# Transposing K on VectorE in place, in 32x32 blocks of element pairs, with block-diagonal queries and one score bank per pair

## Chip, cores and metric

The kernel runs on one core of a Trainium2 chip. The metric is the device time of one execution in microseconds, a median over several executions.

## The reference

Two layers share one K/V cache. Each is attention of one new token per batch row over 8192 cached keys, with a residual, then a silu feed-forward with a residual. A layer norm stands before each part.

```python
B, Sq, D = 8, 1, 512
Hq, Hkv, Sk, Dh = 32, 8, 8192, 128            # 4 query heads share a KV head
# all arrays bf16; F = 1792

q = (x @ wq) as heads
scores = einsum("bhqd,bhkd->bhqk", q, k) * (Dh ** -0.5)
o = einsum("bhqk,bhkd->bhqd", softmax(scores), v)
attention = o @ wo

x = x + attention(layernorm(x));  x = x + silu_ffn(layernorm(x))
x = x + attention(layernorm(x));  x = x + silu_ffn(layernorm(x))   # same K, V, weights
```

K and V of one batch row and KV head (a "pair") are 2 MB each. There are 64 pairs, each used in both layers, so 128 visits.

## The kernel before

The core does the batch rows in an interleaved order. K and V come in units of 512 KB (a quarter of a pair each) into an arena in on-chip memory, and a few units of each row are kept from the first layer for the second. Four "slots" make a pair, one per unit of K. Between the slots, the steps of a row's projection, feed-forward and next queries (a "middle") are slipped in, one step at a time. A helper records every read and write of a buffer and emits the waits.

```python
UNIT = 2048; NUNIT = 23; NKTR = 2; KEEP = 16
# ... cut ...
def k_src(b, g, q):
    return A_k_cache[b, g].rearrange("(p c) d -> p c d", p=128)[:, 16 * q:16 * q + 16, :]
def v_src(b, g, q):
    return A_v_cache[b, g].rearrange("(p c) d -> p c d", p=128)[:, 16 * q:16 * q + 16, :]
# ... cut ...
def layernorm():                                  # twice in each middle
    # ... bn_stats, bn_aggr on DVE, cut ...
    op(pool, lambda: pool.tensor_scalar(ve[0:B, :], mv[0:B, 1:2], LN_EPS, None, op0=ALU.add), ...)
    op(pool, lambda: pool.tensor_tensor(rstd[0:B, :], ve[0:B, :], mhalf[0:B, :], ALU.pow), ...)
# ... cut ...
def do_transposes(n, q):                          # a unit of K, as 1024 pairs of bf16
    # ... choice of the destination, kept unit or ring, cut ...
    src = unit(u).bitcast(FP32)
    for half in range(2):
        mm([lambda m=m: pe.transpose(TP[half][:, 128 * m:128 * m + 128],
                                     src[:, (4 * half + m) * 128:(4 * half + m + 1) * 128], ident[:, :])
            for m in range(4)], reads=[r_unit[u], res("ident")], writes=[r_TP[half]])
        if half == 0:
            op(dve, lambda: dve.tensor_copy(o, i), reads=[r_TP[half]], writes=[r_half, r_dst])
        else:
            op(act, lambda: act.copy(o, i), reads=[r_TP[half]], writes=[r_half, r_dst])
    free.append(u)

def do_scores(n, q):                              # 4 matmuls of 512 keys, 8 query columns
    # ... cut ...
    pe.matmul(SC[bk][32 * j:32 * j + 2 * REP, :], Q[:, b, g, e, :],
              kv[:, i * 512:(i + 1) * 512, e], start=(e == 0), stop=(e == 1))

def do_exp(n):
    # nb = -scale * max, on DVE, cut
    for t in range(2):                            # two score banks per pair
        op(act, lambda t=t, bk=bk: act.activation(P[:, t, :], SC[bk][:, :], ACT.Exp,
               bias=nb[:, :], scale=SM_SCALE, accum_out=ss[:, t:t + 1]), ...)

def do_pt(n):
    # 8 matmuls P x selection -> PTP; DVE copies PTP to PT; 2 f32 matmuls sum the sums; DVE: rz = 1 / sum
def do_pv(n, v):
    # 4 matmuls PT x V unit -> PV, accumulated over the four units
def do_norm():
    op(act, lambda: act.activation(E[:, :], PV[:, :], ACT.Copy, scale=rz[:, :]), ...)
def do_combine(n):
    # 4 f32 matmuls, 8 PE instructions: add the four partial outputs
    op(dve, lambda: dve.tensor_copy(attn[:, g * REP:(g + 1) * REP, b], MISC[:, 0:REP]), ...)

for slot in range(4 * NP + V_LAG + 1):            # program order of one slot
    # pump(): issue every load whose unit is free
    # scores of the slot before (plus max, exp at a pair's end), a middle step,
    # transposes of this slot, a middle step, P's transposition (slot 2), PV, norm, combine
```

## Time and profile before

| | before |
|---|---|
| median when the prediction was made (3 runs) | 1968.27 us |
| profiled span, mean granted TensorE clock | 1936.7 us, 0.904 |
| distance of the all-reduces in quiet pairs (the pair time) | 13.6 to 13.7 us |
| extra time of one middle | 26 us |
| bytes loaded | 481.9 MB |

The prediction below shows the lines that carry its argument. The groups of before's page give, after the bar, busy time and mean ns of one instruction, then the idle time before them and what ended most of it. The exp of 512 scores takes 682 ns, and the f32 combine is a group of 1024 PE instructions, eight per pair:

```profile
L643 ACT ACTIVATE P<-SC,nb 128x512 bf16<-128x512 f32 x256 | 173.5, 682 | 362.4 <-DVE junk L634 276.9
...
L693 PE MATMUL MISC<-selc,E 128*128 128x4 f32 x1024 | 138.6, 259 | 3.3 <-DVE hsT L512 2.5
```

The view of windows gives each engine's busy time in a stretch, then the granted TensorE clock, the DMA share and the rate. One quiet pair (one without a middle's steps and without kept units) of before has PE busy for 9.62 of 13.66 us, at the full clock:

```profile
1000.00:1013.66 13.66, 9.62 (x87) 5.97 (x86) 5.26 (x14) 4.27 (x9) 0.37 (x1) 1.00 0.94 351
```

### The profile page before, as it was taken

The numbers are of one execution on the slowest core, as the hardware profiler recorded it, in microseconds if no ns is written. First come the engines' busy times: TensorE is split into PE (matmuls) and PEld (weight loads), VectorE is DVE, ScalarE is ACT, GpSimd is POOL, SyncE is SP. The second block draws the span as 40 slices with busy tenths as digits, with TensorE's granted clock in tenths as the row PEclk, the third lists the DMA queues.
The fourth block names the chain that finished last, engine by engine and source line by source line (L and its number), as shares of the span: only waits on it lengthen the run. The fifth ranks groups of instructions, "written<-read, shape, count | busy, mean of one in ns | idle before, by whom it ended". The sixth has DMA issues, their size and how long they took to land. (4 is left out here: it accounts for less than half of the span.)

```text
span 1936.7 us, 30341 instructions
## 1 busy us (share of the span) xinstructions
PE 1373.5 (71%) x11410; PEld 822.5 (42%) x11410; DVE 701.5 (36%) x1789; ACT 542.7 (28%) x1150; POOL 64.9 (3%) x174
## 2 busy tenths in 40 slices
PE   3776787677767677766777767767676767767776
PEld 1444344444444344443444444444444444444443
DVE  3333333333333333333333323333333333333332
ACT  1332223322232223232233323332223322322331
POOL 0000000000000000000000000000000000000000
PEclk9998879988999888997899978899799988997997
DMA  9975697756977569765796658966598756855970
GB/s 380 374 268 167 214 352 258 235 163 218 383 251 235 179 234 371 235 220 180 261 390 220 214 162 313 339 224 205 167 337 326 241 164 209 301 176 185 361 277 1
DMA packets 135408, 483.84 MB, mean 250 GB/s; under 512 B 14417, under 2 KB 20321, under 8 KB 135009
## 3 DMA queue, kind: packets, MB, share of 16 engines
q1 hardware_dynamic: 135264, 481.89, 71.9%
q8 instruction: 94, 1.54, 0.3%
q14 instruction: 50, 0.40, 0.1%
HBM read 481.83 MB, written 0.01 MB: 249 GB/s over the span
## 5 line engine op out<-in xcount | busy, mean ns | idle before, releaser
L574 PE MATMUL TP<-ident,arena 128*128 128x128 f32 x3584 | 551.3, 303 | 0.0
L574 PEld LDWEIGHTS TP<-ident,arena 128*128 128x128 f32 x3584 | 436.2, 154 | 221.7 <-issue 221.7
L599 PE MATMUL SC<-ktring,Q 128*8 128x512 bf16 x1536 | 258.1, 418 | 328.2 <-ACT ktring L585 325.8
L585 ACT COPY ktring<-TP 128x512 int32<-128x512 int32 x384 | 224.4, 584 | 796.1 <-PE PV L677 368.7
L583 DVE COPY ktring<-TP 128x512 int32<-128x512 int32 x384 | 263.7, 687 | 345.2 <-PE TP L574 345.0
L612 DVE TENSOR_REDUCE m<-SC 128x1 f32<-128x512 f32 x256 | 176.8, 690 | 327.2 <-PE SC L599 327.1
L643 ACT ACTIVATE P<-SC,nb 128x512 bf16<-128x512 f32 x256 | 173.5, 682 | 362.4 <-DVE junk L634 276.9
L677 PE MATMUL PV<-arena,PT 128*16 128x512 bf16 x2048 | 231.1, 410 | 10.7 <-PE PV L677 0.3
L599 PEld LDWEIGHTS SC<-ktring,Q 128*8 128x8 bf16 x1536 | 37.4, 83 | 423.0 <-ACT ktring L585 418.4
L693 PEld LDWEIGHTS MISC<-selc,E 128*128 128x128 f32 x1024 | 127.5, 196 | 32.8 <-DVE rz L664 27.5
L693 PE MATMUL MISC<-selc,E 128*128 128x4 f32 x1024 | 138.6, 259 | 3.3 <-DVE hsT L512 2.5
L599 PE MATMUL SC<-arena,Q 128*8 128x512 bf16 x512 | 91.8, 448 | 60.6 <-ACT arena L585 60.6
L627 POOL PARTITION_ALL_REDUCE mall<-mh x128 | 47.7, 373 | 1700.6 <-DVE mh L620 1700.6
L677 PEld LDWEIGHTS PV<-arena,PT 128*16 128x16 bf16 x2048 | 53.5, 86 | 96.0 <-issue 73.1
L652 PE MATMUL PTP<-selp,P 128*128 128x32 bf16 x1024 | 67.3, 179 | 32.8 <-ACT P L643 26.1
L687 ACT ACTIVATE E<-PV,rz 128x512 f32<-128x512 f32 x128 | 88.4, 691 | 5.1 <-PE PV L677 5.1
L698 DVE CAST attn<-MISC 128x4 bf16<-128x4 f32 x128 | 22.6, 176 | 169.2 <-PE MISC L693 169.2
L660 PE MATMUL MISC<-ss,sameh 128*128 128x1 f32 x512 | 75.6, 251 | 8.2 <-DVE CH L417 8.2
L652 PEld LDWEIGHTS PTP<-selp,P 128*128 128x128 bf16 x1024 | 51.5, 98 | 65.2 <-ACT P L643 39.2
L395 PE MATMUL MISC<-identb,xn 8*128 8x8 bf16 x72 | 5.2, 175 | 96.1 <-DVE xn L385 96.1
L660 PEld LDWEIGHTS MISC<-ss,sameh 128*128 128x128 f32 x512 | 67.6, 192 | 8.8 <-ACT CH L416 8.8
L585 ACT COPY arena<-TP 128x512 int32<-128x512 int32 x64 | 37.4, 584 | 109.7 <-PE PV L677 85.4
(64 smaller groups left out, 571.2 us busy)
## 6 DMA issues: line engine op xcount, KB each, us to landing
arena<-in_A_k_cache_dram SPq DMA_DIRECT2D x448, 512.0 KB, 5.8
arena<-in_A_v_cache_dram SPq DMA_DIRECT2D x448, 512.0 KB, 4.8
wq<-in_A_wq_dram SPq DMA_DIRECT2D x1, 4096.0 KB, 16.0
wo<-in_A_wo_dram SPq DMA_DIRECT2D x1, 4096.0 KB, 18.1
w<-in_B_w_dram SPq DMA_DIRECT2D x2, 1792.0 KB, 16.5
X<-in_A_x_dram SPq DMA_DIRECT2D x1, 8.0 KB
out_dram<-X SPq DMA_DIRECT2D x1, 8.0 KB
```

The costliest lines, as they stand in the source:

```text
L574: [lambda m=m: pe.transpose(TP[half][:, 128 * m:128 * m + 128], src[:, (4 * half + m) * 128:(4 * half + m + 1) * 128], ident[:, :]) for m ...
L583: op(dve, lambda: dve.tensor_copy(o, i), reads=[r_TP[half]], writes=[r_half, r_dst])
L585: op(act, lambda: act.copy(o, i), reads=[r_TP[half]], writes=[r_half, r_dst])
L599: lambda e=e, i=i, j=j, bk=bk: pe.matmul(SC[bk][32 * j:32 * j + 2 * REP, :], Q[:, b, g, e, :], kv[:, i * 512:(i + 1) * 512, e], start=(e = ...
L612: op(dve, lambda: dve.tensor_reduce(mm2[:, t:t + 1], SC[bk][:, :], AX.X, ALU.max), reads=[r_SC[bk]], writes=[res(f"m2_{n % 2}_{t}")])
L627: lambda: pool.partition_all_reduce(mall[:, :], mh[:, 1, :], 128, bass.bass_isa.ReduceOp.max),
L643: lambda t=t, bk=bk: act.activation(P[:, t, :], SC[bk][:, :], ACT.Exp, bias=nb[:, :], scale=SM_SCALE, accum_out=ss[:, t:t + 1]),
L652: [lambda t=t, x=x: pe.matmul(PTP[:, (4 * t + x) * 32:(4 * t + x + 1) * 32], P[:, t, x * 128:(x + 1) * 128], sel_p[:, :], start=True, stop ...
L660: [lambda t=t: pe.matmul(MISC[:, 0:1], same_h[:, :], ss[:, t:t + 1], start=(t == 0), stop=(t == 1)) for t in range(2)],
L677: lambda x=x: pe.matmul(PV[32 * x:32 * x + 16, :], PT[:, 4 * t + x, 8 * j0:8 * j0 + 16], vv[:, :, x, :], start=(v == 0), stop=(v == 3),)
L687: op(act, lambda: act.activation(E[:, :], PV[:, :], ACT.Copy, scale=rz[:, :]), reads=[r_PV, res("rz")], writes=[res("E")])
L693: [lambda s=s: pe.matmul(MISC[:, 0:REP], E[:, s * 128:(s + 1) * 128], sel_c[:, s * REP:(s + 1) * REP], start=(s == 0), stop=(s == 3)) for ...
```

## The change

Before, each K unit made a round trip: PE transposes it into PSUM, DVE and ACT copy it back, PE scores it. The change lets one DVE instruction transpose the unit where it lies (128x1024 int32). The kernel is written for a transposition in 32x32 blocks of 4-byte elements (pairs of bf16); that the instruction works so is taken as given. In this layout each group of 32 partitions holds its own keys, so the queries are laid out block-diagonally and a unit takes 16 small score matmuls. All 8192 keys of a pair now fit one score bank, so there is one max and one exp per pair. For P to come out in an order that V can follow, the exp writes its result permuted, and V's units are mapped differently in memory. The sum over partitions moves from PE to a second all-reduce on POOL. The division moves from before the combine to after it. The freed ring makes room for two more arena units and a seventeenth kept unit.

```diff
-NUNIT = 23
-NKTR = 2
-KEEP = 16
+NUNIT = 25
+KEEP = 17
 ... cut: buffers, banks, constants, and the layout of Q ...
     def v_src(b, g, q):
-        return A_v_cache[b, g].rearrange("(p c) d -> p c d", p=128)[:, 16 * q:16 * q + 16, :]
+        return A_v_cache[b, g].rearrange("(a p c) d -> a p c d", a=4, p=128)[q]
 ... cut: V_LAG 6 -> 5, wq first in the load queue ...
             def do_transposes(n, q):
-                for half in range(2):
-                    ... 4 PE transposes into TP[half], one copy by DVE or ACT ...
-                free.append(u)
+                v = unit(u).bitcast(I32)
+                op(dve, lambda: dve.transpose(v, v), reads=[r_unit[u]], writes=[r_unit[u]])
             def do_scores(n, q):
-                ... 4 matmuls: 8 query columns x 512 keys ...
+                for i in range(4):
+                    for j in range(4):
+                        pe.matmul(sc[32 * j:32 * j + 16, :, q, :], Q[:, b % 3, g, :, :, i // 2, i % 2],
+                                  kv[:, :, j, i // 2, :, i % 2], start=(i == 0), stop=(i == 3))
             def do_exp(n):
-                for t in range(2):
-                    act.activation(P[:, t, :], SC[bk][:, :], ACT.Exp, ..., accum_out=ss[:, t:t + 1])
+                act.activation(P[:, :].rearrange("r (x p c) -> r x c p", x=4, c=4),
+                               SC[n % 2].rearrange("r (x c p) -> r x c p", x=4, c=4),
+                               ACT.Exp, ..., accum_out=ss[:, :])
             def do_pt(n):
-                ... 8 matmuls for P, 2 f32 matmuls of the sums, reciprocal ...
+                ... 4 matmuls for P ...
+            def do_pt_out(n):
+                dve.tensor_copy(PT, PTP); dve.tensor_scalar(zh, sel_h, ss, op0=mult)
+                pool.partition_all_reduce(zall, zh, 128, add)
+            def do_z(n):
+                dve.reciprocal(rz[n % 2], zall)
-                op(act, lambda: act.activation(E[:, :], PV[:, :], ACT.Copy, scale=rz[:, :]), ...)
+                op(act, lambda: act.copy(E[:, :], PV[:, :]), ...)
-                dve.tensor_copy(attn[:, g * REP:(g + 1) * REP, b], MISC[:, 0:REP])
+                dve.tensor_tensor(attn[:, g * REP:(g + 1) * REP, b], CMB[:, 0:REP], rz[n % 2][:, :], ALU.mult)
 ... cut: the slot loop. New order in a slot: transpose, middle step, exp (slot 0), P's matmuls (slot 1),
     scores, max (slot 3), PT's copy (slot 1), reciprocal (slot 2), PV, combine and attn's product ...
```

## The prediction

> **What bounds the kernel now.** I read the page first, then the timeline of a quiet stretch, then the waits of the compute engines and of the load queue, then the starts of the 128 all-reduces (one per pair of batch row and KV head, so their distances are the pair times). From the page, the busy shares, the load on the DMA engines and its rate in 40 slices:
>
> ```profile
> PE 1373.5 (71%) x11410; PEld 822.5 (42%) x11410; DVE 701.5 (36%) x1789; ACT 542.7 (28%) x1150; POOL 64.9 (3%) x174
> ...
> DMA  9975697756977569765796658966598756855970
> GB/s 380 374 268 167 214 352 258 235 163 218 383 251 235 179 234 371 235 220 180 261 390 220 214 162 313 339 224 205 167 337 326 241 164 209 301 176 185 361 277 1
> ```
>
> No engine is full on average. The DMA engines are full (share 9, about 380 GB/s) only in some slices, after kept buffers were given back; elsewhere they run at 160 to 260. So memory is not the bound. The timeline shows a loop between engines:
>
> ```profile
> 1003.58 0.62 PE L599 MATMUL SC<-ktring,Q 128*8 128x512 bf16 x4 [2.46 <-ACT ktring L585]
> ...
> 1004.12 1.09 PE L574 MATMUL TP<-ident,arena 128*128 128x128 f32 x8
> 1004.82 0.69 DVE L583 COPY ktring<-TP 128x512 int32<-128x512 int32 x1 [2.65 <-PE TP L574]
> ...
> 1005.14 0.39 PE L677 MATMUL PV<-arena,PT 128*16 128x512 bf16 x4
> ...
> 1005.62 0.58 ACT L585 COPY ktring<-TP 128x512 int32<-128x512 int32 x1 [2.09 <-PE PV L677]
> ...
> 1006.26 0.62 PE L599 MATMUL SC<-ktring,Q 128*8 128x512 bf16 x4 [0.72 <-ACT ktring L585]
> ```
>
> A K unit (512 KB, a quarter of a pair) is transposed on PE (1.09 us), copied out by DVE (0.69) and ACT (0.58), and only then scored; PE stands still for the copies. The four score groups of a pair are 2.68, 3.88, 2.68 and 4.42 us apart (the long ones hold P's transposition with the combine, and the two exps ahead of ACT's copy): 13.66 us. The waits say the same, those of the load queue too, which waits for PE to release a buffer:
>
> ```profile
> PEld SC L599 <- ACT ktring L585: 418.4, 267, 3.7
> ...
> DVE ktring L583 <- PE TP L574: 345.0, 195, 3.6
> ```
> ```profile
> SPq L70 <- PE TP L574: 1137.2, 405, 8.2
> ```
>
> The all-reduces are 13.6 to 13.7 us apart in quiet pairs, about 7.1 in the 16 pairs whose K and V are kept from the first pass, and 15.55, 25.51, 25.22 and 14.52 in the four that hold a batch row's projection, FFN and next queries (a "middle"): 80.8 against 4 x 13.66 = 54.6, so a middle costs 26 us extra. There are eight. One part of it is POOL changing its configuration between the all-reduce and the layer norm:
>
> ```profile
> L377 POOLq MODIFY_POOL_CONFIG  x34: 82/85/85, 173.4 to 1906.3; - x34
> L377 POOL TENSOR_SCALAR ve<-mv x18: 223/252/253, 9.1 to 1923.5; 8x1 f32<-8x1 f32 x18
> its engine sat idle before it (us, times) until:
>   issue: 133.2, 16
> ```
>
> 133.2 / 16 = 8.3 us before each layer norm inside the kernel, with its input ready.
>
> [...] PSUM to SBUF, the 256-element cast took 424 ns and the 512-element reduction 690, thus 1.04 ns per element. [...] four 128x512 PV matmuls took 0.39 us in all, though one has a mean of 410 ns. [...]
>
> **The change, part by part.** *K.* One DVE instruction transposes a unit in place, 1024 int32 per partition in 32x32 blocks. [...] It removes 1.09 us of PE, 0.69 of DVE and 0.58 of ACT per unit and two handovers. Each 32-partition quadrant now holds its own keys, so the queries become block diagonal (16 columns) and a unit takes 16 matmuls of 128 columns instead of 4 of 512. Four PV weight loads took 0.10 us, 25 ns each; with as much per matmul, 32 x 25 = 0.8 us per unit (an estimate[...]).
>
> *One bank per pair.* One max (0.69) and one exp (0.69 and 0.19 for the sum) instead of two each, four matmuls for P instead of eight, no f32 matmul of the sums (0.58 us of PE). In its place a small DVE product (0.22, like the mask row) and a second all-reduce, off the path: 0.5 us from its input to its reader.
>
> *Buffers.* 25 units, 17 kept, where there were 23 with 16 kept and a ring of 2. A kept K needs no second unit. Loads fall from 896 to 1024 - 8 x 17 = 888. V keeps 512 KB transfers, now contiguous: no gain assumed.
>
> *A full pair.* DVE in program order, from the end of the mask row (0): T0 to 1.28; the bias (0.24, its all-reduce is back at 0.5) to 1.5; T1 to 2.75. ACT's exp runs from 1.55 to 2.43, P's four matmuls to 2.85, PT's copy 2.9 to 3.3, product to 3.5. Now DVE meets the attention output, which needs in PE's order: scores of unit 1 (to 3.65), PV's first group, and the combine (1.06 us): 5.0. DVE waits 1.5 us there. Then 5.2; T2 to 6.45, reciprocal 6.6, T3 7.85, scores of unit 3 (0.8) 8.65, max 9.35, mask row **9.6 us**. Busy DVE is 4 x 1.24 + 2.15 = 7.1 of it, waits for PE 2.5. PE has about 4 x 0.8 + 4 x 0.39 + 0.35 + 1.06 = 6.2 us of work. The transfer of 4.19 MB takes 11.0 us at 380 GB/s, so memory and DVE are now close. But kept pairs load nothing while the queue runs ahead.
>
> *Other pairs.* Kept ones have no T: PE's chain, about 6.8 us (7.1 before). Those with one kept K unit: 8.4.
>
> *A middle.* Same steps. POOL changes configuration before the layer norm and again after it; pairs now have an all-reduce every 5 us, so the second change, hidden before (15 us or more to the next all-reduce), shows partly. I add 3 us for each of two: 26 + 6 = 32.
>
> *Ends.* wq is first in the queue now, and the first all-reduce comes near 37 instead of 47.6 us. But the first eight pairs need 33.6 MB and 12.1 MB of weights: 45.7 / 0.38 = 120 us, so the eighth ends near 122. From the last all-reduce to the end: 30.8 before, 29 now.
>
> *Sum.* 122 + 96 full pairs x 9.6 (922) + 8 x 8.4 (67) + 16 x 6.8 (109) + 8 x 32 (256) + 29 = **1505 us**.
>
> **Rivals.** *Transposition at half rate* [...]: 1.07 us more for each of 440 units, +470: 1975, no change. [...] One in fifteen. *Memory becomes the bound:* 465.6 + 12.1 MB at 380 GB/s are 1257 us, with both ends 1290; with the eight middles, when only eight units are free (11 us of loads) and the queue runs dry, about 1400. For it: a full pair needs 11.0 us of transfer against 9.6 of DVE. It is the lower end if DVE's waits are shorter than I count. *PE's clock falls:* [...] PE could be granted the low clock, as in kept pairs, where the score group took 1.02 to 1.06 us instead of 0.62. Then scores and combine on DVE's path add about 2 us per pair: 1710. Against it: quiet stretches had 1.00 at 70% busy PE, and PE keeps 65%. *POOL:* if each layer norm blocks two all-reduces fully, 8 x 10 us more: 1585.
>
> **Range and chances.** Most of the uncertainty is in the pair: 1 us more or less is 104 us. A pair of 8.6 us meets the memory bound near 1400; one of 11 gives 1650. Range 1400 to 1650. It stays over 2% slower or equal only if the transposition is slow or something stalls in each unit: 0.92 faster, 0.05 within 2%, 0.03 slower.
>
> **What would show it.** Right: the DVE transposition at 1.2 to 1.3 us, x440; all-reduces in quiet pairs 9 to 11 us apart; DVE the busiest engine near 70% and its largest waits for the combine and the score group; the DMA mean near 320 GB/s; ACT below 25%. Wrong: transpositions above 2 us; a score group above 1.2 us; DVE waiting for landings rather than PE in most pairs (then memory is the bound and the middles set the rest); middles costing much over 32 us.

The forecast came to 1505 us. The 1240 ns of one transposition: only the slope of 1.04 ns per element in it was measured. Its terms stand in the forecast and in its sum, as 1.24 to 1.28 us for each T and so 4 x 1.24 us in each full pair's 9.6, and one T less in the 8.4; read them as the author's estimate. The 3 us added for each of two changes of POOL's configuration are also the author's estimate, against 8.3 us measured for one. For the rival of the clock, in before's pair with kept units (499.24 to 506.44 us) the mean granted clock was 0.74, and 0.50 during the two score groups of 1.06 and 1.02 us.

## The result

| | before | after |
|---|---|---|
| median | 1957.38 us (4 runs, 1944.85 to 1971.95) | 1589.0 us (4 runs, 1586.04 to 1591.59) |
| mean granted TensorE clock | 0.904 | 0.581 |
| pair time in quiet stretches | 13.6 to 13.7 us | 10.27 to 10.31 us |
| pair time where K and V are kept | about 7.1 us | 6.7 to 7.9 us |
| extra time of one middle | 26 us | 29.8 to 33.5, mean 31.5 us |
| first all-reduce | 47.6 us | 30.67 us |

The ratio is 0.8115, with a 95% interval of 0.8041 to 0.819. The change is faster, and the time lies inside the predicted range, 84 us above the predicted 1505.

The page of after, busy shares, the granted clock in tenths over 40 slices, and GB/s in the same slices:

```profile
PE 931.2 (59%) x14026; PEld 529.4 (33%) x14026; DVE 795.6 (50%) x1649; ACT 277.1 (17%) x494; POOL 120.5 (8%) x302
...
PEclk9997555555555565555655555555655555555555
...
GB/s 378 389 404 298 211 390 408 304 208 248 399 409 258 187 292 410 408 213 179 340 409 408 186 185 371 408 344 199 217 397 408 293 207 252 334 199 188 393 377 1
```

PE lost 442 us of work and ACT half of its own, as intended. Nothing on average is full. New is the second line: TensorE is mostly at half clock. The 9997 at its start is not evidence of a faster clock: after's trace holds no clock record before 134.8 us, the view shows 1.00 up to there, and all eight combines before then took 1.87 us, as they do later at 0.50. So the mean of 0.581 is somewhat too high; from 134.8 us on it is 0.54. The groups of the same page:

```profile
L541 DVE STREAM_TRANSPOSE arena<-arena 128x1024 int32<-128x1024 int32 x440 | 536.9, 1230 | 18.6 <-DMA arena<-in_A_k_cache_dram 18.3
...
L582 ACT ACTIVATE P<-SC,nb 128x512 bf16<-128x512 f32 x128 | 181.6, 1419 | 1000.4 <-DVE junk L575 900.9
...
L638 PE MATMUL CMB<-selc,E 128*128 128x4 f32 x1024 | 233.3, 351 | 0.7 <-ACT E L633 0.7
L645 DVE TENSOR_TENSOR attn<-CMB,rz 128x4 bf16<-128x4 f32 x128 | 22.5, 176 | 303.7 <-PE CMB L638 303.7
L562 DVE TENSOR_REDUCE mx<-SC 128x1 f32<-128x512 f32 x128 | 88.0, 688 | 103.3 <-PE SC L552 103.3
```

The transposition takes 1230 ns and hardly ever waits for its data (18.3 us in the whole run). The exp takes 1419 ns for 512 elements, twice before's 682. DVE waits 303.7 us for the combine and 103.3 us for the scores. A quiet pair shows where; the timeline gives start, duration and, in brackets, idle time before and its releaser:

```profile
834.28 0.23 DVE L564 TENSOR_SCALAR mh<-mask,mx 128x4 f32<-128x4 f32 x1
834.42 1.24 DVE L541 STREAM_TRANSPOSE arena<-arena 128x1024 int32<-128x1024 int32 x1
...
835.63 1.24 DVE L541 STREAM_TRANSPOSE arena<-arena 128x1024 int32<-128x1024 int32 x1
...
835.80 1.40 ACT L582 ACTIVATE P<-SC,nb 128x512 bf16<-128x512 f32 x1 [8.45 <-DVE junk L575]
...
837.26 0.39 PE L592 MATMUL PTP<-selp,P 128*128 128x64 bf16 x4 [0.51 <-ACT P L582]
...
837.69 0.42 DVE L599 CAST PT<-PTP 128x256 bf16<-128x256 f32 x1 [0.82 <-PE PTP L592]
...
838.70 1.87 PE L638 MATMUL CMB<-selc,E 128*128 128x4 f32 x8
...
840.61 0.17 DVE L645 TENSOR_TENSOR attn<-CMB,rz 128x4 bf16<-128x4 f32 x1 [2.36 <-PE CMB L638]
840.69 1.23 DVE L541 STREAM_TRANSPOSE arena<-arena 128x1024 int32<-128x1024 int32 x1
...
843.17 0.61 PE L552 MATMUL SC<-arena,Q 128*16 128x128 bf16 x16 [0.15 <-DVE arena L541]
...
843.83 0.69 DVE L562 TENSOR_REDUCE mx<-SC 128x1 f32<-128x512 f32 x1 [0.72 <-PE SC L552]
```

DVE walks through its program in order and stops three times: 0.82 us for P's matmuls (behind the exp), 2.36 us for the combine, 0.72 us for the last scores. That is 3.9 of 10.3 us. The next transposition stands behind the second stop, with its data ready. The window of this pair:

```profile
834.60:844.90 10.30, 6.42 (x92) 3.75 (x92) 6.37 (x13) 1.83 (x3) 0.82 (x3) 0.50 1.02 406
```

The clock is 0.50, and the DMA engines move 406 GB/s at a busy share of 1.02, full. A pair needs 4.19 MB, thus 10.3 us at that rate. From this picture alone, memory could be the bound just as well as DVE's stops; only experiments part the two.

In a middle, POOL stands still for nothing visible, more often than in before (24 such waits in after, 16 in before). Its timeline in after, around one of them:

```profile
900.44 0.25 POOL L364 TENSOR_SCALAR ve<-mv 8x1 f32<-8x1 f32 x1 [10.18 <-DVE mv L363]
900.77 0.59 POOL L366 TENSOR_TENSOR rstd<-ve,mhalf 8x1 f32<-8x1 f32 x1
907.93 0.39 POOL L568 PARTITION_ALL_REDUCE mall<-mh  x1 [6.57 <-issue]
...
931.47 0.25 POOL L364 TENSOR_SCALAR ve<-mv 8x1 f32<-8x1 f32 x1 [8.67 <-issue]
931.80 0.59 POOL L366 TENSOR_TENSOR rstd<-ve,mhalf 8x1 f32<-8x1 f32 x1
938.58 0.44 POOL L605 PARTITION_ALL_REDUCE zall<-zh  x1 [6.19 <-issue]
```

"issue" is time in which the engine waited for nothing that the profile shows. POOL's sequencer has its configuration instructions there: 34 before the layer norm's arithmetic, 18 and 16 before the two all-reduces. Over the run, the waits for nothing visible before the layer norm's arithmetic are 68.1 us over 8 (8.5 each), those before the two all-reduces 53.7 over 8 (6.7) and 47.8 over 8 (6.0). So in these cases a layer norm costs a change there and a change back.

### The profile page after: what moved, and what is told of

The parts are those of the page before. It is cut to its first block, busy times and chain, and to the rows that moved or that the text cites. A ratio compares the mean times of both kernels' runs of the same rounds, so it can differ in the third digit from the quotient of the medians.

```text
span 1585.1 us, 33836 instructions
## 1 busy us (share of the span) xinstructions
PE 931.2 (59%) x14026; PEld 529.4 (33%) x14026; DVE 795.6 (50%) x1649; ACT 277.1 (17%) x494; POOL 120.5 (8%) x302
## 5 line engine op out<-in xcount | busy, mean ns | idle before, releaser
L552 PE MATMUL SC<-arena,Q 128*16 128x128 bf16 x8192 | 314.0, 298 | 425.5 <-DVE junk L575 203.0
L541 DVE STREAM_TRANSPOSE arena<-arena 128x1024 int32<-128x1024 int32 x440 | 536.9, 1230 | 18.6 <-DMA arena<-in_A_k_cache_dram 18.3
L552 PEld LDWEIGHTS SC<-arena,Q 128*16 128x16 bf16 x8192 | 176.5, 113 | 596.1 <-DVE junk L575 261.1
L582 ACT ACTIVATE P<-SC,nb 128x512 bf16<-128x512 f32 x128 | 181.6, 1419 | 1000.4 <-DVE junk L575 900.9
L623 PE MATMUL PV<-arena,PT 128*16 128x512 bf16 x2048 | 319.9, 605 | 9.9 <-DVE PT L599 9.4
L638 PEld LDWEIGHTS CMB<-selc,E 128*128 128x128 f32 x1024 | 222.9, 321 | 54.9 <-issue 53.7
L638 PE MATMUL CMB<-selc,E 128*128 128x4 f32 x1024 | 233.3, 351 | 0.7 <-ACT E L633 0.7
L645 DVE TENSOR_TENSOR attn<-CMB,rz 128x4 bf16<-128x4 f32 x128 | 22.5, 176 | 303.7 <-PE CMB L638 303.7
L562 DVE TENSOR_REDUCE mx<-SC 128x1 f32<-128x512 f32 x128 | 88.0, 688 | 103.3 <-PE SC L552 103.3
L568 POOL PARTITION_ALL_REDUCE mall<-mh x128 | 47.6, 372 | 799.8 <-DVE mh L564 746.1
L599 DVE CAST PT<-PTP 128x256 bf16<-128x256 f32 x128 | 53.9, 421 | 107.9 <-PE PTP L592 107.8
L605 POOL PARTITION_ALL_REDUCE zall<-zh x128 | 55.1, 431 | 480.0 <-DVE zh L601 432.3
L633 ACT COPY E<-PV 128x512 f32<-128x512 f32 x128 | 81.8, 639 | 5.1 <-PE PV L623 5.1
L592 PEld LDWEIGHTS PTP<-selp,P 128*128 128x128 bf16 x512 | 29.8, 119 | 153.9 <-ACT P L582 152.0
```

Source lines behind the costliest of these rows:

```text
L541: op(dve, lambda: dve.transpose(v, v), reads=[r_unit[u]], writes=[r_unit[u]])
L552: lambda i=i, j=j: pe.matmul(sc[32 * j:32 * j + 16, :, q, :], Q[:, b % 3, g, :, :, i // 2, i % 2], kv[:, :, j, i // 2, :, i % 2], start=(i ...
L562: op(dve, lambda: dve.tensor_reduce(mx[:, :], SC[n % 2][:, :], AX.X, ALU.max), reads=[r_SC[n % 2]], writes=[res("mx")])
L568: lambda: pool.partition_all_reduce(mall[:, :], mh[:, :], 128, bass.bass_isa.ReduceOp.max),
L582: lambda: act.activation(P[:, :].rearrange("r (x p c) -> r x c p", x=4, c=4), SC[n % 2].rearrange("r (x c p) -> r x c p", x=4, c=4), ACT.E ...
L592: [lambda x=x: pe.matmul(PTP[:, 64 * x:64 * x + 64], P[:, 128 * x:128 * x + 128], sel_p[:, :], start=True, stop=True) for x in range(4)],
```

## The experiments

The theory after reading the traces (A): a quiet pair is DVE's own work plus three stops, and the largest, for the combine, is an accident of program order. The rivals: (B) memory sets 10.3 us per pair; and, beside these, the half clock on PE and the permuted exp as what makes the stops long. POOL's configuration is a separate theory for the middles, and the V mapping one for the memory rate. Before's median moved (1957.38, 1966.76 and 1949.32 us), so gains given against after's 1589.0 are good to some 10 us; the profiled spans of the first three repairs (1585.1 against 1415.7, 1521.0 and 1511.2 us) give nearly the same sizes.

The comparison with the reference accepted all eight kernels, even the three that mix up keys and values. So at this tolerance it does not prove that the order of keys is right.

### Attention's product read later

The combine is no longer read in the slot that computes it but two slots later, after the last transposition. With it, the start of the next middle's bookkeeping moves two slots later; nothing else changes, and the result stays right.

```diff
-                op(dve, ... attn = CMB * rz ...)          # right after the combine's matmuls
+            def do_attn(n): op(dve, ... attn = CMB * rz ...)
+                pa = v_at(slot - 1 - 2)                   # after this slot's transposition
+                if pa and pa[1] == 3:
+                    do_attn(pa[0])
```

> The changed kernel, but DVE reads the combine two slots later (after the fourth transposition of the pair instead of before the third); nothing else moves, results stay right. Theory A (a quiet pair is the in-order chain of DVE and PE): DVE's wait of 2.36 us per pair for the combine goes, a quiet pair falls from 10.30 to 8.6-8.9 us wherever loads are ahead, and the total to 1420-1480 us. Theory B (memory is the bound already: 4.19 MB at the 408 GB/s of full slices are 10.28 us, the pair's 10.30): the pair stays at 10.3, DVE waits for landings instead, total 1575-1590.

Measured: 1414.87 us (1413.15 to 1417.47), ratio 0.7193 (0.7148 to 0.7238), before 1966.76. Quiet pairs take 8.46 to 8.50 us. The timeline of one:

```profile
754.92 1.87 PE L638 MATMUL CMB<-selc,E 128*128 128x4 f32 x8
...
756.83 0.17 DVE L648 TENSOR_TENSOR attn<-CMB,rz 128x4 bf16<-128x4 f32 x1
...
758.24 0.69 DVE L562 TENSOR_REDUCE mx<-SC 128x1 f32<-128x512 f32 x1 [1.23 <-PE SC L552]
```

The combine still takes 1.87 us, but DVE transposes meanwhile and no bracket stands at the product. The stop for the scores grew from 0.72 to 1.23 us, so 1.8 of the 2.36 us are saved. Theory A holds, and B falls as the bound of after: at 8.5 us a pair consumes faster than memory delivers. This works only because the queue runs ahead in kept pairs and middles; the first pairs, where nothing runs ahead, are at 10.2 us here. Moving one small instruction brings 174 us, which is more than all that went wrong in the prediction.

### Exp written in natural order

```diff
-                        P[:, :].rearrange("r (x p c) -> r x c p", x=4, c=4),
-                        SC[n % 2].rearrange("r (x c p) -> r x c p", x=4, c=4),
+                        P[:, :], SC[n % 2][:, :],
```

The result is wrong: P's order no longer matches V's.

> The changed kernel with the exp writing P in the order in which it reads the scores (wrong result on purpose; amount of work unchanged). Theory A: the exp took 1.40 us for 512 columns because of its permuted write, and returns to 0.69 as before the change; PT's copy, PV and the combine start about 0.7 us earlier, the pair is 9.6 us, total 1510-1530. Rival: the exp is hidden beside the second transposition: pair within 0.2 us of 10.3, total above 1570. Theory B: 1575-1590 too, with DVE waiting for landings.

Measured: 1523.24 us (1519.56 to 1527.56), ratio 0.7748 (0.7705 to 0.7791). Quiet pairs take 9.70 us. The group on its page:

```profile
L582 ACT ACTIVATE P<-SC,nb 128x512 bf16<-128x512 f32 x128 | 88.0, 688 | 973.5 <-DVE junk L575 866.1
```

The permuted writing doubled the activation, from 688 to 1419 ns. It costs 0.6 us per pair, 66 us in all. ACT is busy for 14% of the time, and still it lies on the path, because DVE's copy of PT waits for it.

### No configuration change on POOL

The layer norm's root is computed on DVE (an integer shift and two Newton steps, nine small instructions that take 1.7 us in this run's timeline, from 864.34 to 866.03 us), so POOL only ever does all-reduces inside the loop. The result stays right.

```diff
-                op(pool, ... ve = mv + eps ...)
-                op(pool, ... rstd = ve ** -0.5 ...)
+                op(dve, ... ve = mv + eps ...)
+                op(dve, ... t = ve >> 1 (as int32) ...); op(dve, ... y = 0x5F3759DF - t ...)
+                for _ in range(2):
+                    ... y = y * (1.5 - 0.5 * ve * y * y), three DVE instructions ...
```

> The changed kernel with the layer norm's reciprocal root on DVE (a shift, two Newton steps: 9 small DVE instructions, about 2 us) instead of two POOL instructions, so POOL runs only all-reduces and never changes its configuration. If the changes of configuration set the middles: the DVE waits of about 5.7 and 8.2 us per middle go, a middle costs 18-22 us extra instead of 31.6, total 1480-1510. Rival (handovers between PE, ACT and DVE set the middles, the POOL waits are taken by others): less than 5 us per middle, total above 1550.

Measured: 1512.56 us (1511.87 to 1512.91), ratio 0.7692 (0.7652 to 0.7732). The four pairs of a middle take, for instance, 16.94, 15.98, 18.01 and 12.42 us, thus 63.4 against 41.2 for four quiet pairs: 22.2 us extra. Over the eight middles the mean is 21.5 us, instead of 31.5. In a middle the all-reduces now wait for DVE's input alone, with no "issue" left:

```profile
866.98 0.37 POOL L580 PARTITION_ALL_REDUCE mall<-mh  x1 [12.75 <-DVE mh L576]
873.15 0.43 POOL L617 PARTITION_ALL_REDUCE zall<-zh  x1 [5.80 <-DVE zh L613]
```

So the changes of configuration cost about 10 us per middle, 80 us in all; the run is 76 us shorter. Before had waits of the same kind (8.3 us at each layer norm), so a part of this gain was probably to be had without the change; that was not tried. The rest of a middle, some 21.5 us, is put down to its own work. One surprise: the first all-reduce came later, at 35.8 us instead of 30.67. A wait of 8.50 us for nothing visible now stands before POOL's first instruction, which starts at 8.99 us instead of 2.06; that this delays the all-reduce is likely, but was not tried.

### The kernel before with V's new mapping

```diff
-        return A_v_cache[b, g].rearrange("(p c) d -> p c d", p=128)[:, 16 * q:16 * q + 16, :]
+        return A_v_cache[b, g].rearrange("(a p c) d -> a p c d", a=4, p=128)[q]
```

Wrong: the rest of before does not follow this order.

> The kernel before with the V mapping of the change alone: each V unit is read as 512 KB in one piece instead of 128 pieces of 4 KB, 16 KB apart (wrong result on purpose; the rest untouched). If the mapping is what raised the rate of full slices from 380 to 408 GB/s: full slices of this run reach 395-410. If it is the changed kernel's timing: they stay at 375-390. In both cases the time should stay within 1% of before, as the kernel before waits for PE and not for memory; if memory set part of it, 2% or more faster.

Measured: 1959.07 us (1949.21 to 1964.93), ratio 0.9958 (0.9897 to 1.002): no difference. Full stretches of 5 us move 406 to 413 GB/s here, 401 to 416 in before and 404 to 410 in after. So contiguous units bring nothing, and the 408 GB/s were there all along. My 380 was read from slices of 48 us that were not full throughout.

### PE kept busy

Two matmuls of 128x512 into an unused bank stand at the end of three of four slots. The result stays right.

```diff
+    WARM = bank("WARM")
+                if 8 <= slot < 4 * NP and q != 2:
+                    mm([lambda: pe.matmul(WARM[:, :], identb[:, :], wq_sb[:, 0, 0:512], start=True, stop=True)
+                        for _ in range(2)], reads=[...], writes=[res("WARM")])
```

> The changed kernel with two full-width matmuls of 512 columns into an unused bank at the end of three of each pair's four slots, where PE waits anyway; results stay right. If PE runs at the low clock because it is used too little, and that clock lengthens DVE's wait for the combine: the granted clock goes from 0.58 to above 0.85, the combine from 1.87 to 1.06 us, the score group from 0.61 to about 0.4, a quiet pair from 10.3 to 9.2-9.6, total 1490-1540. If the clock doesn't come back (too little, or another cause): the combine stays at 1.87 and the total at 1585-1640. If the clock comes back and the time stays: the clock is not on the path.

Measured: 1564.92 us (1560.44 to 1568.16), ratio 0.8016 (0.7984 to 0.8048), with a mean clock of 0.645 only. The aim of a clock above 0.85 was missed. Still the run decides, since pairs of both kinds stand side by side in it:

```profile
core 0: us, PE busy (x) PEld busy (x) DVE busy (x) ACT busy (x) POOL busy (x), PEclk, DMA share, GB/s
797.20:806.40 9.20, 6.40 (x99) 2.87 (x98) 6.40 (x13) 1.83 (x3) 0.84 (x3) 0.85 1.03 408
806.40:816.90 10.50, 8.99 (x99) 4.18 (x98) 6.29 (x13) 1.85 (x3) 0.76 (x2) 0.50 1.03 411
```
```profile
801.00 1.05 PE L639 MATMUL CMB<-selc,E 128*128 128x4 f32 x8
...
802.09 0.18 DVE L646 TENSOR_TENSOR attn<-CMB,rz 128x4 bf16<-128x4 f32 x1 [1.33 <-PE CMB L639]
...
810.73 1.87 PE L639 MATMUL CMB<-selc,E 128*128 128x4 f32 x8
...
812.64 0.17 DVE L646 TENSOR_TENSOR attn<-CMB,rz 128x4 bf16<-128x4 f32 x1 [2.36 <-PE CMB L639]
```

The pair at the higher clock takes 9.13 to 9.15 us, against 10.3 without dummies and 10.55 with them at half clock. So the clock matters, in kind as the prediction's rival said: against after's pair without dummies the half clock costs 1.15 us (1.4 within this run, where dummies stand in both pairs; the warm pair is itself at 0.85 only), about 0.8 of it in the combine, and DVE's stop shrinks by 1.03. It is not a separate bound: in the first experiment the combine took 1.87 us as well, and DVE had no idle time in front of its product.

What decides the clock I could not find from busy shares. The cold pair above has PE busy for 86% of the time, the warm one for 70%. The quiet pair of after shown above has 62% at 0.50, and no idle time in front of a PE row of it is above 1.78 us. The quiet pair of before has 70% at 1.00, with idle time of up to 2.46 us in front of a PE row. The runs show which clock was granted in these stretches; what grants it was not shown.

### No transposition

```diff
-                op(dve, lambda: dve.transpose(v, v), reads=[r_unit[u]], writes=[r_unit[u]])
```

Wrong (the scores use K untransposed). The question was what would bound the kernel if K cost DVE nothing.

> The changed kernel without the DVE transpositions (wrong result on purpose; every other instruction stays). DVE loses 537 us of work. If the transpositions lie fully on the chain of a quiet pair: pairs fall to the chain of kept pairs, 7 to 8 us, until memory takes over: 4.19 MB per full pair at the 408 GB/s of full 5 us stretches are 10.3 us, 477.7 MB 1171 us; with both ends and the eight middles 1270-1360 us in all. If they are mostly hidden beside waits: above 1450.

Measured: 1438.78 us (1432.04 to 1448.07), ratio 0.7374 (0.7332 to 0.7416). The expectation of 1270 to 1360 was missed. Quiet pairs do fall to 6.7 to 7.9 us while loads are ahead, then meet memory at 10.2:

```profile
PEld SC L552 <- DMA arena<-in_A_k_cache_dram: 129.2, 116, 12.6
...
PEld PV L623 <- DMA arena<-in_A_v_cache_dram: 87.5, 95, 2.3
```

These are waits for landings that after did not have. The middles hardly moved (for instance 23.5, 12.97, 23.9 and 9.43 us), and there memory idles, most likely because only eight units circulate while the other 17 are kept (argued, not tried with another number):

```profile
660.00:700.00 40.00, 19.36 (x380) 10.88 (x384) 8.62 (x34) 7.63 (x18) 2.87 (x7) 0.67 0.51 165
```

In the 40 us of this middle the rate is 165 GB/s. I had taken memory (477.7 MB at 408 GB/s, 1171 us) and the middles as if they overlapped; they add up for the most part. Taking out 537 us of DVE work brings only 150 us, less than moving one instruction does: the stops stay (DVE waits 346.7 us for the combine in this run), and pairs then meet memory.

### Three repairs together

The first and third edits as above. The exp is made plain in a way that keeps the result right: the score matmuls write into the bank with a step of four elements, so that the exp's order is already P's.

```diff
-                sc = SC[n % 2].rearrange("p (x c s) -> p x c s", x=4, c=4)
+                sc = SC[n % 2].rearrange("p (x s c) -> p x c s", x=4, c=4)
-                        P[:, :].rearrange("r (x p c) -> r x c p", x=4, c=4),
-                        SC[n % 2].rearrange("r (x c p) -> r x c p", x=4, c=4),
+                        P[:, :], SC[n % 2][:, :],
```

> Three mends of the changed kernel together, results right: DVE reads the combine two slots later; the layer norm's root on DVE; and the scores are written to their bank in the order in which P is needed (the matmuls' output strided by 4 elements), so that the exp reads and writes in one order. If gains add: quiet pairs 7.7-8.0 us, middles about 20 extra, total 1290-1350, and memory the bound in long stretches (408 GB/s, DVE waiting for landings). If the strided output slows the score matmuls (group above 0.9 us instead of 0.61): pairs above 8.5, total above 1370.

Measured: 1354.41 us (1349.71 to 1357.93), ratio 0.6945 (0.6914 to 0.6976), just outside the expected range. Against after this is 235 us less, where the three single gains sum to 174 + 66 + 76 = 316. The traces show two things that take a part of the difference; how much each takes was not measured. Memory is met: quiet pairs take 7.03 us while loads are ahead, then 10.2, and DVE now waits for K to land. Writing with a step also has its price on PE, the score group taking 0.62 us at the full clock, against 0.42 in the first half of the warm pair of the run with dummies.

```profile
L564 PE MATMUL SC<-arena,Q 128*16 128x128 bf16 x8192 | 444.3, 393 | 315.4 <-DVE junk L587 167.2
```
```profile
DVE arena L553 <- DMA arena<-in_A_k_cache_dram: 115.6, 112, 10.2
```
```profile
531.00:556.00 25.00, 16.95 (x344) 10.69 (x332) 21.38 (x44) 4.09 (x9) 2.83 (x7) 1.00 1.03 408
586.00:606.00 20.00, 14.51 (x172) 9.48 (x176) 12.38 (x23) 2.73 (x6) 1.60 (x4) 0.50 1.03 408
```

In the first stretch DVE is busy for 21.38 of 25 us: here it is the bound at last, as the change intended. In the second, memory is.

### Four repairs

On top of these, the combine's operands are bf16: ACT writes the partial outputs as bf16, and the four f32 matmuls (eight PE instructions) become four.

```diff
-    sel_c = sb([128, 16], FP32, "selc")
+    sel_c = sb([128, 16], BF16, "selc")
-                op(act, lambda: act.copy(E[:, :], PV[:, :]), reads=[r_PV], writes=[res("E")])
+                op(act, lambda: act.copy(Eb[:, :], PV[:, :]), reads=[r_PV], writes=[res("Eb")])
```

> As the three mends, and the combine in bf16 ([...] 0.5-0.9 us instead of 1.87 at the low clock); results right within the tolerance. The combine is off DVE's path by then but still ahead of the scores in PE's order: 0 to 30 us faster than the three mends, 1270-1345; no difference if memory sets the time there.

The 0.5 to 0.9 us was the author's estimate.

Measured: 1333.82 us (1329.96 to 1336.65), ratio 0.6832 (0.6805 to 0.686). It is the fastest kernel, 16% below after and 32% below before. The combine falls from 1.05 to 0.25 us at the full clock, and DVE's wait for K to land grows from 115.6 to 157.4 us, so that a part of the time regained goes there:

```profile
DVE arena L556 <- DMA arena<-in_A_k_cache_dram: 157.4, 150, 10.1
```

Its quiet pairs while loads are ahead stay at 7.02 us, with a clock of 1.00 at a PE busy share of 55%. Beside after's 0.50 at 62%, this once more says that the busy share alone does not decide the clock.

## Why the prediction was right, and where it was off

The direction, the size and the mechanism were right: the loop between PE, DVE and ACT went, and a DVE chain with stops for PE took its place. By the steps of the prediction:

- *The transposition*, predicted at 1240 ns, took 1230, x440. The half-rate rival, 1.07 us more for each, is out.
- *A full pair*, predicted at 9.6 us, took 10.3. This is the step that was mis-sized; 96 x 0.7 = 67 of the 84 us. Counted from the end of the mask row (834.51) as in the prediction, the terms compare like this:

| step | predicted us | measured us |
|---|---|---|
| second transposition ends | 2.75 | 2.36 |
| exp with its sum ends | 2.43 | 2.70 |
| PT's copy ends | 3.3 | 3.60 |
| combine starts | 3.94 | 4.19 |
| combine ends | 5.0 | 6.06 |
| third and fourth transpositions end | 7.85 | 8.60 |
| next mask row ends | 9.6 | 10.28 |

- In that table, the f32 combine was put at before's 1.06 us and took 1.87 at the half clock: 0.81 of the 1.06 us by which it ended late. The exp was put at 0.69 + 0.19 us and took 1.40 + 0.26: I took the permuted writing as free, which nothing in the profile of before had shown. Going the other way, consecutive DVE instructions here start before the one before them ends (in the pair above, the bias at 835.58 and the second transposition at 835.63 us, while the first ends at 835.66; with this the second ended 0.4 us earlier than predicted), and the score group took 0.61 us, not 0.8. The measured gains of removing one cost alone, 0.6 us for the exp and 1.15 us for the clock, are larger than the 0.7 that the pair was off by. So an optimism in these terms was partly made up by a pessimism in others.
- *The rival of the clock* came true, against my reason that 70% busy had meant 1.00 and PE would keep 65%. PE kept 62% in quiet pairs and got 0.50. I had put the rival at 2 us per pair; it is 1.15.
- *Memory* was predicted close behind, and it was: the rate was 408 GB/s instead of 380, so a pair's loads take 10.28 us, not 11.0. That equals the pair time by coincidence; two kernels with shorter pairs on the same loads show that memory does not hold after's pair.
- *Where DVE waits*: for the combine and the scores, as said (303.7 and 103.3 us), and also for P's matmuls (107.8), which I had at almost nothing because of the exp. DVE busy near 70% was wrong: it is 50% in all and 62% in a quiet pair, since the stops are longer and the middles dilute it. So PE, at 59%, is the busiest engine of after, and not DVE. The DMA mean is 303 GB/s, predicted 320; ACT is at 17%, as said.
- *Pairs with kept units* took 7.5 on average and 9.97 us, predicted 6.8 and 8.4. They hold the same combine and exp. This is 24 us of the sum.
- *A middle*: 31.5 measured, 32 predicted, 26 before. The removal of POOL's configuration gave about 10 us per middle.
- *The ends*: the first all-reduce is at 30.67 us (predicted near 37), the eighth all-reduce is at 114.8 us (predicted 122), and from the last all-reduce to the end are 30 us (predicted 29).

The sum with measured terms: 114.8 + 96 x 10.3 + 8 x 9.97 + 16 x 7.5 + 8 x 31.5 + 30 = 1585 us, against a profiled span of 1585.1. That the total came within 6% owes something to luck: the late exp and combine, the early transposition and score group, and the early start are errors of opposite sign.

What the prediction did not see at all is the largest lever: the stop for the combine was counted as 1.5 us and accepted, where reading the product two slots later removes it. What switches TensorE's clock stays open: no run tests its cause.

## What to carry to other kernels

After taking a round trip between engines away, walk through the in-order program of the engine that is left and ask of each small instruction that reads another engine's result what stands behind it; moving such a reader later can be worth more than removing a large piece of work (here 174 us, against 150 for taking the whole transposition away). Price an instruction with the access pattern that it will have, not with that of its old form (here 1419 ns for the exp with its permuted write, against 688 without). Clocks, memory and stops did not add up as single costs here (235 us for three repairs together, 316 as the sum of their single gains): test the repairs alone and together.
